# A clustered attention and a feed-forward layer on one core: five hand-over queues written in a new order

## The chip, the cores and the metric

The kernel runs on one core of one Trainium2 chip. The time is device time of that core in microseconds, the median of the runs shown; lower is better. A core has five instruction queues that run on their own and wait for each other by semaphores: TensorE (PE; its weight loads are PEld), VectorE (DVE), ScalarE (ACT), GpSimd (POOL) and SyncE (SP), which here issues nearly all transfers.

## The reference

For 4 batches and 8 heads of 768 tokens with 64 numbers each, every query and key is given to the nearest of 16 centroids; a query sees only keys of its own cluster. The attention's output (3072 rows of 512) goes through a feed-forward layer of width 1024.

```python
mask = q_assign[:, :, :, None] == k_assign[:, :, None, :]
scores = np.where(mask, scale * q @ k.T, -1e9)
attn = softmax(scores) ; x = (attn @ v) as rows of 512
h = x @ w_in
solu = h * softmax(h)
ln = (solu - mean) / np.sqrt(var + 1e-06) * g_ln
return ln @ w_out
```

## The kernel before

The 32 heads are taken as 16 pairs, named batch.pair (0.0 to 3.3). For a pair, queries and keys (side 0 and 1) are loaded, turned so that the head dimension lies on partitions, scored against the centroids, and written in bf16 with a one-hot cluster code below them. With the code in the contraction, a score of a foreign cluster lies so far below that its exponential is nothing; the mask costs no instruction of its own. Score blocks of 512 (in the first pair 384) columns go through three PSUM banks: TensorE writes a bank, ScalarE takes the exponential into one of nine SBUF tiles, TensorE multiplies these with the values, and VectorE divides by the row sums. There are 294 such banks. Each of 24 blocks of 128 rows then goes through the feed-forward layer. It is folded: the output weights are centred and scaled once (ce), so that a row block needs a maximum, an exponential with its sum, a product u, a transposing transfer of u, the variance, one factor alpha for each row, and a last scaling.

Nothing of the order is left to a scheduler. The kernel registers about 1800 small steps with `add(name, engine, cost, key, fn, needs, ...)`, and class `Weave` (L18) holds for each engine a text, `ORDER`, that gives the kinds of steps in queue order with repeat counts: `S3 V` is three score steps and a value step, each the next of its kind. A word such as `=ca0.1.1.1` names one step out of turn. `AWAY` names steps that run on another engine than their default. `run()` then walks the five queues and emits the instructions; the real waits come from the tiles that the instructions touch. An engine's queue is strict: an instruction that waits holds all behind it.

The steps that are spoken of below, by kind:

- `ld`, `lv` (L410, L413, L382, L539): loads of queries or keys, and of values. From batch 1 on, one side of a pair is loaded in four quarters (ld1.2.1.0, .1, .2, and the last, ld1.2.1). `lo`, `li` (L576, L560): loads of the output and input weights.
- `tp` (PE, L394) and `xa` (L401): in batch 0 the turning by TensorE and the copy out of PSUM. `xt` (DVE, L419): from batch 1 on, the turning by VectorE.
- `cl` (PE, L462), `tb`, `mx`, `oh`, `ot` (DVE, L471 to L506), `pl` (L518, L526; some by SyncE, L524), `bl` (memset, L535): cluster scores, their maximum, the one-hot code, and its placing. `zo` (L893) is one memset for it.
- `ca` (L443 on ScalarE, L445 and L447): cast of one head of queries or keys to bf16; ca1.3.1.1 is batch 1, pair 3, keys, second head. `cv` (L544): cast of values. `wi` (L563): cast of a quarter of the input weights. `z`, `sg`, `gs` are small preparations.
- `S` (PE, L613), `E` (ACT, L619), `V` (PE, L636), `N` (DVE, L648 and L661): scores, exponentials, values, division.
- For row block f: `tx` (SP, L691) turns x by a transfer; `h` (PE, L722, four steps, h2.1.0 is block 2, second half, first part); `hm` (DVE, L728), `ex` (ACT, L734), `u` (DVE, L741), `tu` (SP, L746, a transposing transfer), `bn` and `ag` (DVE, L752, L756), `at` and `al` (POOL, L762 to L771), `y` (PE, L786, four steps), `sc` (L801 on ScalarE, L803 on VectorE), `ou` (SP, L813). In the last blocks `ptx` and `ptu` turn on TensorE.

Two bindings matter for the order. The product u of block f frees a PSUM bank that h of block f+1, second half, writes, so the loop h, hm, ex, u runs through three engines. And one PSUM bank is shared by cl and y: it is handed on by tb or sc.

Of the kernel before, what the change touches and what calls it, by code (L numbers as in the profile page):

```python
# [22 lines left out]
class Weave:  # L23
# [3 lines left out]

    ORDER = {}
    ORDER["SP"] = """
        ld4 lv si ld4 lv lg ld4 lv2 ld4 lo2 ld4 lo ld3 lo ld3 li4 tx ld3 lv3 tx ld4 tu ld9 lv ld tu  # L30
        tx ld3 tu ld3 ou ld2 ou ld tu ld12 tu ld4 lv ld2 ou tx ld3 tu ou ld2 tx lv ld tu ld4 tx ld
        tu ou2 ld lv ld4 tu ld4 tu ld ou ld7 pl ou ld lv2 ld3 tu lv tx ou tu lv pl ld4 ou2 tx lv tu
        tx ou tu pl2 tu2 tx tu tx ou2 tx ou tu tx2 ou tu2 ou2 tu2 ou6
    """
    ORDER["POOL"] = """
        po z ca2 pl2 cv z bl pl2 ca z ca pl2 ca z2 ca3 cv ca cv ca pl3 sg ca cv2 pl3 ca2 gs pl ca cv
        ca wi ca pl2 wi3 bl ca pl2 cv at cv pl ca pl al bl at cv ca pl ca pl cv ca3 al at ca al ca
        at ca pl2 bl cv pl2 ca4 at ca2 al ca pl2 bl pl2 cv2 ca3 al at pl2 bl pl2 ca pl al ca3 at cv
        at pl ca pl2 ca2 pl al cv2 bl cv2 pl2 ca pl al pl at al at pl2 ca3 at al bl cv pl2 bl cv2
        ca3 pl5 al cv3 at al ca2 cv ca cv ca2 at ca2 pl ca al pl2 at2 pl3 at ca cv al at2 al2 at2 al  # L40
        at al3 at al2 at2 al2
    """
    ORDER["PE"] = """
        wm tp fl3 cp fl2 tp2 cl tp fl10 cl fl8 S3 tp2 S2 tp S cq S tp S2 tp2 S2 V3 S cl S tp2 V3 S gt S tp S
        tp S2 cl S2 V2 S V S2 tp S2 tp S2 V2 S V S2 cl S2 V2 S V2 S3 V S2 V2 S2 V S cl S3 su S2 V3 S
        V S3 V3 S2 V S su S2 V S V3 S3 me S3 V4 S3 cl S3 V4 S2 h S h S2 h S h S2 V3 S2 V h S h V S V
        S h S V S V S h S2 V3 S2 V h S2 h V2 S y3 S2 h3 S3 y V3 h V S2 V2 S cl S3 h2 S2 V3 S y2 S V
        h2 S V y2 S h S V h S2 h S y3 S2 y V3 h S3 cl V2 S V S y S2 y2 S3 V3 S y S2 V3 S2 cl S V S2
        V2 S h S2 V2 S V S h S2 V2 cl V2 S3 y2 S V S2 V y S2 y V2 S3 h2 S V h S h S2 V h S V S V y2
        S h V y2 S2 V S h3 S cl V S2 V2 S h V cl S3 h2 V y V S3 y2 V S h V3 S y S h S2 h2 S3 V2 y h  # L50
        S V S2 y V3 y S3 h3 y S3 V3 S h S V S V cl S V S h S cl V2 S3 y V2 S y S2 y V2 S3 h y V S3 V
        h V2 S3 cl S2 V2 S y3 S2 y S V3 S V S y S2 V S V3 S2 y2 S3 y V2 S2 h V2 S3 h3 S V S2 V y S V
        h2 V2 S y S2 y V y S h2 S3 cl h V S2 V3 S h V2 S3 h2 S y S2 V h S2 V y2 V4 S3 y h S2 h V h V
        S V S y2 S3 V3 h2 S2 h2 S2 y2 S V S h2 S V3 S2 h S h S2 V S y V2 S V y2 S2 h2 S2 h2 V2 S2 V2
        y S2 h V2 h V S2 h S V h S3 V2 h y S V y3 V h3 S2 y3 S2 y h2 V2 h y h y3 h V h V y4 h ptx h
        y4 h2 y3 h2 y ptu2 y6 ptu y ptu y5
    """
    ORDER["DVE"] = """
        cn cb xa ca tb mx oh ot pl2 tb mx oh ot xa3 bl cf cv xa zo xa2 tb ca mx oh gk N ot tb pl mx
        xa2 oh xa cv N ot tb pl N xt mx xt N oh ot tb pl2 ca N pl xt mx N sk oh N ot xt ce3 N tb ce5  # L60
        N hm mx N u oh ot bn N bn ag hm xt2 u N bn2 hm ag sc xt u N bn tb hm mx bn oh ag u xt bn ot
        xt N cv hm bn ag sc xt tb mx N u xt oh ot sc N bn2 xt ag xt tb N hm mx tb N oh ot u xt mx N
        bn oh bn xt hm ot ag N cv u bn2 xt hm tb mx u N tb oh mx hm ot bn2 oh ag u N sc ag hm bn ot
        u bn N xt2 ag xt2 hm tb N bl mx tb bn2 oh u N xt ag xt sc hm ot tb mx oh N bn sc N u bn N ag
        xt ot bn ca N mx sc oh hm u bn ag N xt hm bn2 bl tb u ot ag N hm mx bn2 u bn N oh ot hm bl2
        u ag N cv hm sc bn u N hm ag bn N bn u bn2 hm ag2 N bn u bn2 N ag hm bn u N ag hm bn2 u bn2
        hm sc u N ag2 bn tx hm bn sc u bn ag hm bn tu ag u2 bn2 ag sc
    """
    ORDER["ACT"] = """
        wa xa2 ca2 xa ca2 E12 xa2 E6 xa E58 ex E12 ex E8 ex E8 ex E3 sc E5 ca E2 ex E25 ex E9 sc E6  # L70
        ex E5 sc E2 ex E9 ex E8 ex E9 sc E6 ex E18 ex E21 ex E5 sc E3 ex E9 ex E7 sc E2 ex E7 ex E8
        ex E7 ex E6 sc E ex E2 sc E3 ex E2 sc ex sc ex sc ex tu sc tu2 sc2 oz
    """
    AWAY = {}
    AWAY.update(dict.fromkeys("""
        ca0.0.0.0.0 ca0.0.0.1.1 ca1.3.1.1 sc23.0 tu22.1 tu23.1 xa0.0.1.0 xa0.2.1.0 xa0.2.1.1
        xa0.3.0.0
    """.split(), "ACT"))
    AWAY.update(dict.fromkeys("""
        bl0.0.1 bl2.2 bl3.1 bl3.2 bl3.3 ca0.0.1.0.0 ca0.1.1.0 ca1.0.0.1 ca3.1.1.0 cv0.0.0 cv0.2.0  # L80
        cv1.2.0 cv2.0.0 cv3.3.0 pl0.0.0.0.1 pl0.1.0.0 pl0.2.1.1 pl0.3.0.0 pl0.3.0.1 pl0.3.1.0 sc0
        sc10 sc13 sc17 sc19 sc2 sc23.1 sc3 sc6 sc8 sc9 tu22.0 zo
    """.split(), "DVE"))
    AWAY.update(dict.fromkeys("""
        ca0.0.1.1.1 pl0.0.0.1.0 pl0.0.1.0.0 pl0.0.1.1.0 pl1.0.0.0 pl1.0.0.1 pl1.0.1.0 pl1.0.1.1
        pl1.1.0.0 pl1.1.0.1 pl1.1.1.0 pl1.1.1.1 pl1.2.0.0 pl1.2.0.1 pl1.2.1.0 pl1.2.1.1 pl1.3.0.0
        pl1.3.0.1 pl1.3.1.0 pl1.3.1.1 pl2.0.0.0 pl2.0.0.1 pl2.0.1.0 pl2.0.1.1 pl2.1.0.0 pl2.1.0.1
        pl2.1.1.0 pl2.1.1.1 pl2.2.0.0 pl2.2.0.1 pl2.2.1.0 pl2.2.1.1 pl2.3.0.0 pl2.3.1.0 pl2.3.1.1
        pl3.0.0.0 pl3.0.0.1 pl3.0.1.0 pl3.0.1.1 pl3.1.0.1 pl3.1.1.0 pl3.1.1.1 pl3.2.0.0 pl3.2.0.1
        pl3.2.1.0 pl3.3.0.1 pl3.3.1.0 pl3.3.1.1  # L90
    """.split(), "POOL"))
    HOP = 0.17
    LANES = 8
# [1178 lines left out]
```

## Time and profile before

| | |
|---|---|
| median of 3 runs | 225.22 us (224.92 to 555.72) |
| span of the profiled execution | 225.3 us |
| granted TensorE clock | 1.00 in the whole span |
| instructions profiled | 6672 |
| transfers | 38.80 MB, 172 GB/s in the mean |
| HBM read and written | 23.11 MB and 6.29 MB |

In the profile a row of a group gives line, engine, operation, output and inputs, shapes, the count, then busy microseconds and the mean nanoseconds of one, then the idle time of the engine just before these instructions and what ended it. A row of the timeline begins with the start and the length in microseconds. A row of the waits names who waited for whom, with the sum, the count and the longest. The ends of matmuls are modelled, and a releaser is inferred from semaphore events: where a wait was for several things, the last is named, and where the one named had long been done, it was another.

### The profile page before, as it was taken

How to read it: one execution, taken by the hardware profiler on the slowest of the kernel's cores; microseconds unless marked ns; L12 is line 12 of the kernel's file. 1: busy time of each engine (PE TensorE's matmuls, PEld its weight loads, DVE VectorE, ACT ScalarE, POOL GpSimd, SP SyncE). 2: the span in 40 equal slices, each digit the busy share in tenths (PEclk: the TensorE clock that was granted, in tenths of full speed). 3: DMA queues.
4: the chain of work that ended last, by engine and by line, in shares of the span. 5: the costliest groups of instructions: out<-in, count | busy, mean ns of one | idle time of the engine just before them, and what ended most of it. 6: DMA issues, size and time to landing. Idle time of an engine off the chain costs nothing.

```text
span 225.3 us, 6672 instructions
## 1 busy us (share of the span) xinstructions
PE 217.0 (96%) x2454; PEld 142.4 (63%) x2454; DVE 197.2 (88%) x359; ACT 191.9 (85%) x372; POOL 127.0 (56%) x247
## 2 busy tenths in 40 slices
PE   8999999999899999999999999999999999999994
PEld 7676646676556657666567657676566676755452
DVE  3899888899799998999998999887999889988982
ACT  3779978999969999998989899998899998984363
POOL 3499833684792999654667752855696502123331
PEclk9999999999999999999999999999999999999999
DMA  6998999999899899899999998887970637266923
GB/s 153 316 318 164 243 173 224 312 217 192 141 179 168 195 134 157 161 204 170 193 215 174 148 172 217 178 154 190 235 114 9 83 57 155 70 139 158 180 87 140
DMA packets 125679, 38.80 MB, mean 172 GB/s; under 512 B 115016, under 2 KB 121168, under 8 KB 125648
## 3 DMA queue, kind: packets, MB, share of 16 engines
q1 hardware_dynamic: 123904, 37.87, 83.0%
q10 hardware_dynamic: 1744, 0.52, 1.0%
q8 instruction: 19, 0.31, 0.6%
q14 instruction: 12, 0.10, 0.2%
HBM read 23.11 MB, written 6.29 MB: 130 GB/s over the span
## 4 chain that ended last, share of the span: by engine, by line
PE 73%; DMA 8%; DVE 7%; SPq 4%; ACT 3%; issue 3%; POOL 1%; DVEq 0%; ACTq 0%; POOLq 0%
PE sps L613 21%; PE hreg L722 16%; PE yps L786 15%; PE ops L636 11%; DMA raw<-in_k_dram 4%; PE csc L462 3%; SPq L413 3%; PE hreg L394 2%; ACT e L619 2%; DMA uT<-u 2%; DMA xT<-x 2%; PE idle_p L831 1%; DVE xt L419 1%; DVE u L741 1%; PE hreg L585 1%
## 5 line engine op out<-in xcount | busy, mean ns | idle before, releaser
L619 ACT ACTIVATE e<-sps 128x512 bf16<-128x512 f32 (+1 forms) x294 | 150.9, 601 | 14.6 <-PE sps L613 12.1
L613 PE MATMUL sps<-qk 80*128 80x256 bf16 (+5 forms) x636 | 93.7, 262 | 1.6 <-ACT e L619 0.6
L613 PEld LDWEIGHTS <-qk 80*128 80x128 bf16 (+1 forms) x636 | 51.7, 97 | 32.4 <-issue 9.4
L636 PEld LDWEIGHTS <-e 128*128 128x128 bf16 x1152 | 49.2, 97 | 13.0 <-issue 1.9
L722 PE MATMUL hreg<-w_in_sb,xT 128*128 128x512 bf16 x192 | 53.0, 379 | 1.4 <-DVE u L741 1.3
L636 PE MATMUL ops<-v,e 128*128 128x65 bf16 x1152 | 53.5, 193 | 0.1
L786 PE MATMUL yps<-w_out_c,uT 128*128 128x512 bf16 x184 | 48.7, 379 | 0.6 <-DMA uT<-u 0.4
L741 DVE TENSOR_TENSOR u<-e_sb,hreg 128x1024 bf16<-128x1024 bf16 (+1 forms) x25 | 29.1, 1167 | 4.6 <-ACT e_sb L734 4.5
L526 POOL COPY qk<-oht 32x384 f32<-32x384 f32 (+1 forms) x50 | 24.4, 488 | 15.3 <-DVE oht L506 12.6
L752 DVE BATCH_NORM_STATS2 bs<-u 128x6 f32<-128x512 bf16 x48 | 31.5, 676 | 0.1
L728 DVE TENSOR_REDUCE nmax<-hreg 128x1 f32<-128x1024 f32 x24 | 29.0, 1209 | 2.5 <-PE hreg L722 2.2
L734 ACT ACTIVATE e_sb<-hreg,nmax 128x1024 bf16<-128x1024 f32 x24 | 27.0, 1124 | 4.5 <-DVE nmax L728 4.4
L445 POOL CAST qk<-xt 64x768 bf16<-64x768 f32 (+1 forms) x31 | 25.9, 836 | 4.8 <-DVE xt L401 3.3
L786 PEld LDWEIGHTS <-uT 128*128 128x128 bf16 x200 | 18.1, 97 | 13.0 <-issue 0.7
L419 DVE STREAM_TRANSPOSE xt<-raw 128x768 f32<-128x768 f32 x24 | 22.9, 957 | 3.2 <-POOL v L544 1.5
L768 POOL TENSOR_SCALAR esq<-es,mv 128x1 f32<-128x1 f32 x24 | 8.6, 358 | 29.5 <-DVE mv L756 21.3
L722 PEld LDWEIGHTS <-xT 128*128 128x128 bf16 x192 | 16.5, 97 | 11.9 <-DVE u L741 2.3
L447 POOL TENSOR_SCALAR qk<-xt 64x768 bf16<-64x768 f32 (+1 forms) x28 | 22.9, 819 | 1.7
L661 DVE TENSOR_TENSOR x<-ops,den 128x256 bf16<-128x256 f32 (+1 forms) x39 | 18.9, 485 | 1.3
L762 POOL TENSOR_SCALAR es<-esum 128x1 f32<-128x1 f32 x24 | 5.3, 223 | 26.1 <-ACT e_sb L734 25.6
L544 POOL CAST v<-vf 128x384 bf16<-128x384 f32 x27 | 13.6, 518 | 2.9 <-DMA vf<-in_v_dram 2.3
L771 POOL TENSOR_TENSOR alpha<-esq,halves 128x1 f32<-128x1 f32 x24 | 13.5, 563 | 2.0
(80 smaller groups left out, 170.0 us busy)
## 6 DMA issues: line engine op xcount, KB each, us to landing
vf<-in_v_dram SPq DMA_DIRECT2D x16, 384.0 KB, 4.6
out_dram<-y SPq DMA_DIRECT2D x23, 256.0 KB, 2.4
raw<-in_q_dram SPq DMA_DIRECT2D x50, 96.0 KB, 3.7
raw<-in_k_dram SPq DMA_DIRECT2D x50, 96.0 KB, 3.5
w_g<-in_moe_w_out_dram SPq DMA_DIRECT2D x4, 512.0 KB, 6.2
w_st<-in_moe_w_in_dram SPq DMA_DIRECT2D x4, 512.0 KB, 6.0
raw<-in_q_dram SPq DMA_DIRECT2D x3, 384.0 KB, 6.6
raw<-in_k_dram SPq DMA_DIRECT2D x3, 384.0 KB, 7.3
```

What stands on the lines that cost most here:

```text
L419: nc.vector.transpose(xt[:], raws[b, p, i][:].rearrange("p j c -> p (j c)"))
L445: VEC[e].tensor_copy(dst, src)
L526: ins = VEC[e].tensor_copy(dst.bitcast(F32), src.bitcast(F32).unsqueeze(1) .to_broadcast([NB, 2, n // 2]))
L613: nc.tensor.matmul(sps_[n, k][:, c0:c0 + w], side(b, h // 2, 1, h % 2, keys)[r], side(b, h // 2, 0, h % 2, slice(s0 * P, s0 * P + w))[r])
L619: nc.scalar.activation(es[n, k][:, :w], sps_[n, k][:, :w], Act.Exp, scale=exp_scale, bias=-exp_scale)
L636: nc.tensor.matmul(opss[g][:, s, :VW], es[n, k][:, c0:c0 + P], v1[slot(b, h // 2)][:, h % 2, kt, :VW], start=(kt == 0), stop=(kt == n_t - 1))
L722: uses(nc.tensor.matmul(hreg[:, at(f, f2)[1], :], xTs[f][:, dc, :], w_in_sb[:, dc, f2 * FF2:(f2 + 1) * FF2], start=(dc == 0), stop=(dc == ...
L728: uses(nc.vector.tensor_reduce(ff[f, "nmax"][:], pair_of(f), axis=AXY, op=Alu.max, negate=True), *both(f))
L734: uses(nc.scalar.activation(ff[f, "e"][:], pair_of(f), Act.Exp, bias=ff[f, "nmax"][:], accum_out=ff[f, "esum"][:]), *both(f))
L741: uses(nc.vector.tensor_tensor(ff[f, "u"][:, at_], ff[f, "e"][:, at_], pair_of(f)[:, at_], op=Alu.mult), *banks)
L752: nc.vector.bn_stats(ff[f, "bs"][:, f2, :], ff[f, "u"][:, f2, :])
L786: ins = nc.tensor.matmul(dst, ff[f, "uT"][:, at(f, f2)[0] * (n_fc // 2) + c, :], w_out_c[:, fc, cols], start=(fc == chunks[0]), stop=(fc = ...
```

## The change

Only the texts `ORDER` and `AWAY` change. The steps, their code, the tiles and the number of buffers are the same. The queues keep their order until the first scores; behind these the order of all five is new, and it names steps out of turn (for GpSimd above all), which the texts before did not. By `AWAY`, ScalarE gains the casts ca0.1.0.0, ca0.2.0.1, ca1.2.1.0, ca2.1.1.0, ca2.3.0.0 and ca3.2.1.0 and gives up ca1.3.1.1 and the copies xa0.2.1.0 and xa0.2.1.1; of the last scalings it gains sc2, 3, 6 and 13 and gives up sc11, 12, 20 and 22, which go to VectorE. VectorE has wi3 and three whole placements in place of five, and six value casts in place of five; three memsets and zo go to GpSimd, which has 55 casts of queries and keys in place of 59. The queues of SyncE and ScalarE follow in full, the others by their beginning, and VectorE's end.

```diff
     ORDER["SP"] = """
-        ld4 lv si ld4 lv lg ld4 lv2 ld4 lo2 ld4 lo ld3 lo ld3 li4 tx ld3 lv3 tx ld4 tu ld9 lv ld tu
-        tx ld3 tu ld3 ou ld2 ou ld tu ld12 tu ld4 lv ld2 ou tx ld3 tu ou ld2 tx lv ld tu ld4 tx ld
-        tu ou2 ld lv ld4 tu ld4 tu ld ou ld7 pl ou ld lv2 ld3 tu lv tx ou tu lv pl ld4 ou2 tx lv tu
-        tx ou tu pl2 tu2 tx tu tx ou2 tx ou tu tx2 ou tu2 ou2 tu2 ou6
+        ld4 lv si ld4 lv lg ld11 lv2 lo4 ld7 li4 tx lv2 tx ld7 tu lv ld8 lv tx tu2 ou ld12 tu ou2
+        ld10 tu ld4 lv tx tu ld6 ou tx ld4 lv tu2 ou2 tx lv ld13 tu ld6 ou pl ld2 lv tu2 ou ld lv
+        ld3 tx ld2 tu ou tx pl ou ld pl ld lv2 tu ou tu lv ou tx pl ou tu2 tx2 ou tx tu2 tx ou2 tu
+        tx ou tu2 ou2 tu ou5
     """
     ORDER["POOL"] = """
-        po z ca2 pl2 cv z bl pl2 ca z ca pl2 ca z2 ca3 cv ca cv ca pl3 sg ca cv2 pl3 ca2 gs pl ca cv
-        ca wi ca pl2 wi3 bl ca pl2 cv at cv pl ca pl al bl at cv ca pl ca pl cv ca3 al at ca al ca
...
+        po z ca2 pl2 bl ca sg pl2 bl cv =ca0.1.1.1 cv =cv0.1.1 =ca0.1.1.0 zo ca z2 =ca0.2.1.0 gs
+        =pl0.1.0.0 pl2 cv ca =pl0.2.0.1 pl =z5 =pl0.2.0.0 ca pl ca2 cv2 =ca0.3.1.1 ca pl2 =pl1.0.1.1
+        wi =ca1.0.0.1 wi2 =ca1.1.1.1 ca z =pl1.0.0.1 =ca1.1.0.0 cv =pl1.0.0.0 pl bl ca =pl1.1.1.1 pl
+        bl pl =ca1.2.0.0 cv =ca1.1.1.0 =cv1.2.0 pl at2 al2 cv =ca1.3.0.0 ca cv =ca1.2.1.1 =cv1.3.0
...
     ORDER["PE"] = """
-        wm tp fl3 cp fl2 tp2 cl tp fl10 cl fl8 S3 tp2 S2 tp S cq S tp S2 tp2 S2 V3 S cl S tp2 V3 S gt S tp S
-        tp S2 cl S2 V2 S V S2 tp S2 tp S2 V2 S V S2 cl S2 V2 S V2 S3 V S2 V2 S2 V S cl S3 su S2 V3 S
-        V S3 V3 S2 V S su S2 V S V3 S3 me S3 V4 S3 cl S3 V4 S2 h S h S2 h S h S2 V3 S2 V h S h V S V
...
+        wm tp fl3 cp fl2 tp2 cl tp fl10 cl fl8 S3 tp2 cq S2 tp S tp S2 tp S tp S tp V3 S2 cl S V3 S2
+        gt tp S tp S2 cl S2 V S V2 S2 tp S3 V2 S V S tp S2 tp S V2 S2 V2 S2 cl S3 V4 S3 cl S V S2 V2
+        S V S2 su S V S V S V2 S3 su S V S2 V3 S2 me S3 cl S3 V3 S V S3 V2 S V S V S2 h S h2 S h S V
...
     ORDER["DVE"] = """
-        cn cb xa ca tb mx oh ot pl2 tb mx oh ot xa3 bl cf cv xa zo xa2 tb ca mx oh gk N ot tb pl mx
-        xa2 oh xa cv N ot tb pl N xt mx xt N oh ot tb pl2 ca N pl xt mx N sk oh N ot xt ce3 N tb ce5
-        N hm mx N u oh ot bn N bn ag hm xt2 u N bn2 hm ag sc xt u N bn tb hm mx bn oh ag u xt bn ot
...
-        hm sc u N ag2 bn tx hm bn sc u bn ag hm bn tu ag u2 bn2 ag sc
+        cn cb xa ca tb mx oh ot pl2 tb mx oh ot xa3 =pl0.0.1.0.1 xa cf pl =xa0.2.1.0 xa2 tb mx N gk
+        xa oh ot tb mx pl oh ot N xa3 xt N cv xt tb mx N oh tb ot ca N cv pl2 mx oh N ot sk xt N xt
+        ce tb ce2 N ce2 wi ce N ce2 hm mx oh N u bn N ot hm xt bn N u bn ag bn xt hm ag sc xt u N tb
...
+        bn ag bn u bn ag N hm bn ag u bn2 hm sc N u ag bn2 hm tx ag sc u bn2 hm tu sc ag u2 bn2 ag
+        sc2
     """
     ORDER["ACT"] = """
-        wa xa2 ca2 xa ca2 E12 xa2 E6 xa E58 ex E12 ex E8 ex E8 ex E3 sc E5 ca E2 ex E25 ex E9 sc E6
-        ex E5 sc E2 ex E9 ex E8 ex E9 sc E6 ex E18 ex E21 ex E5 sc E3 ex E9 ex E7 sc E2 ex E7 ex E8
-        ex E7 ex E6 sc E ex E2 sc E3 ex E2 sc ex sc ex sc ex tu sc tu2 sc2 oz
+        wa xa2 ca2 xa ca2 E9 ca E3 ca E6 xa E58 ex E11 ex E11 ex E3 ca E7 ex E6 sc E3 ex sc E12 sc
+        E13 ex E11 sc E3 ex E =ca2.3.0.0 E2 sc E2 ex ca E8 ex E3 sc E7 ex E6 sc E11 ex E17 ex E21 ex
+        E8 ex E3 ca E5 ex E9 ex E8 ex E7 sc ex E7 ex E2 sc E5 ex E2 sc E3 ex sc E ex sc ex2 tu sc
+        tu2 sc oz
     """
     AWAY = {}
...
-        ca0.0.0.0.0 ca0.0.0.1.1 ca1.3.1.1 sc23.0 tu22.1 tu23.1 xa0.0.1.0 xa0.2.1.0 xa0.2.1.1
-        xa0.3.0.0
+        ca0.0.0.0.0 ca0.0.0.1.1 ca0.1.0.0 ca0.2.0.1 ca1.2.1.0 ca2.1.1.0 ca2.3.0.0 ca3.2.1.0 sc23.0
+        tu22.1 tu23.1 xa0.0.1.0 xa0.3.0.0
     """.split(), "ACT"))
...
-        bl0.0.1 bl2.2 bl3.1 bl3.2 bl3.3 ca0.0.1.0.0 ca0.1.1.0 ca1.0.0.1 ca3.1.1.0 cv0.0.0 cv0.2.0
-        cv1.2.0 cv2.0.0 cv3.3.0 pl0.0.0.0.1 pl0.1.0.0 pl0.2.1.1 pl0.3.0.0 pl0.3.0.1 pl0.3.1.0 sc0
-        sc10 sc13 sc17 sc19 sc2 sc23.1 sc3 sc6 sc8 sc9 tu22.0 zo
+        bl1.2 bl2.1 ca0.0.1.0.0 ca1.0.1.0 ca3.2.0.1 cv0.2.1 cv0.3.1 cv2.3.1 cv3.0.0 cv3.1.0 cv3.2.1
+        pl0.0.0.0.1 pl0.0.1.0.1 pl0.1.0.1 pl0.3.0.1 pl0.3.1.1 sc0 sc10 sc11 sc12 sc17 sc19 sc20 sc22
+        sc23.1 sc8 sc9 tu22.0 wi3
     """.split(), "DVE"))
```

## What the change does to the time: the prediction

> **What bounds the kernel now.** I read the page's totals first, then TensorE's groups with the shapes kept apart, a short stretch of its timeline, the busy times by stage, and last the waits.
>
> ```profile
> span 225.3 us, 6672 instructions
> PE 217.0 (96%) x2454; PEld 142.4 (63%) x2454; DVE 197.2 (88%) x359; ACT 191.9 (85%) x372; POOL 127.0 (56%) x247
> ...
> L636 PE MATMUL ops<-v,e 128*128 128x65 bf16 x1152 | 53.5, 193 | 0.1
> L722 PE MATMUL hreg<-w_in_sb,xT 128*128 128x512 bf16 x192 | 53.0, 379 | 1.4 <-DVE u L741 1.3
> L786 PE MATMUL yps<-w_out_c,uT 128*128 128x512 bf16 x184 | 48.7, 379 | 0.6 <-DMA uT<-u 0.4 <-DVE cst L471 0.2
> L613 PE MATMUL sps<-qk 80*128 80x256 bf16 x288 | 47.5, 272 | 1.1 <-ACT e L619 0.6
> L613 PE MATMUL sps<-qk 96*128 96x256 bf16 x180 | 29.5, 272 | 0.0
> ...
> 150.34 0.53 PE L636 MATMUL ops<-v,e 128*128 128x65 bf16 x12
> 150.70 0.60 PE L613 MATMUL sps<-qk 80*128 80x256 bf16 x4
> 151.14 0.60 PE L722 MATMUL hreg<-w_in_sb,xT 128*128 128x512 bf16 x2
> ```
>
> The mean length of a matmul holds a tail that the next one overlaps. Two of 512 columns take 0.60 together and 0.379 alone, so the second starts 0.22 after the first; four of 256 columns give (0.60 - 0.272) / 3 = 0.11, and twelve value matmuls (0.53 - 0.193) / 11 = 0.031. In such slots the three large kinds need 376 x 0.22 + 468 x 0.11 + 1152 x 0.031 = 83 + 51 + 35 = 169 us; the other 458 matmuls (transposes, clusters, warming) come on top. So TensorE is the fullest engine, though a gap shorter than the tail is hidden in its 217.
>
> ```profile
> 9.40:55.40 46.00, 44.69 (x544) 29.66 (x545) 41.16 (x84) 41.81 (x88) 30.43 (x54) 1.00 0.97 237
> 55.40:66.00 10.60, 9.28 (x108) 6.27 (x107) 8.98 (x15) 8.35 (x17) 8.64 (x15) 1.00 0.83 141
> 66.00:200.00 134.00, 133.10 (x1576) 88.54 (x1575) 122.88 (x212) 124.83 (x239) 77.65 (x146) 1.00 0.86 155
> 200.00:225.30 25.30, 21.93 (x154) 11.66 (x151) 19.52 (x31) 12.11 (x21) 7.08 (x18) 1.00 0.57 142
> ...
> PE hreg L722 <- DVE u L741: 1.3, 1, 1.3
> ...
> ACT e L619 <- PE sps L613: 12.1, 23, 2.1
> ```
>
> After the stretch and its length the columns are PE, PEld, DVE, ACT, POOL, then the granted clock, which is 1.00 throughout: no term comes from it. From 66 to 200 TensorE is busy 133.1 of 134.0, ScalarE 124.8, VectorE 122.9. Three engines are nearly full and hand work to each other in queues of fixed order. TensorE's visible waits are few: one of 1.3 us, and in the groups above 0.6 for exponentials and 0.4 for a transfer. ScalarE's 12.1 us are its wait for scores, so it is the one that has room, in many small pieces.
>
> **The one wait that the new order plainly removes.** It stands in the second stretch.
>
> ```profile
> 54.39 2.35 SPq L746 DMA_TRANSPOSE uT<-u  x1
> 56.79 0.59 SPq L413 DMA_DIRECT2D raw<-in_k_dram  x1
> ...
> 58.87 0.27 ACT L734 ACTIVATION_READ_ACCUMULATOR e_sb<-hreg,nmax 128x1 f32 x1
> ...
> 60.01 0.98 DVE L419 STREAM_TRANSPOSE xt<-raw 128x768 f32<-128x768 f32 x1 [1.55 <-POOL v L544]
> 60.92 1.18 DVE L741 TENSOR_TENSOR u<-e_sb,hreg 128x1024 bf16<-128x1024 bf16 x1
> ...
> 62.16 1.04 PE L722 MATMUL hreg<-w_in_sb,xT 128*128 128x512 bf16 x4 [1.32 <-DVE u L741]
> ```
>
> The last quarter of a key load leaves SyncE at 56.79, because the transposing transfer tu0 held the queue for 2.35 us ahead of it. VectorE stands 1.55 us before xt1.2.1 (the view names GpSimd, whose cast has nothing to do with that tile; the load is the likely releaser). u1 is queued behind it, though its exponentials were done at 58.87 + 0.27 = 59.14, and h2.1.0 on TensorE waits for u1. The new VectorE queue reads xt1.2.0 bn0.1 N11 u1 bn1.0 ag0 bn1.1 xt1.2.1: u1 no longer stands behind the load. It could start at 59.14 rather than 60.92, 1.78 earlier, against a wait of 1.32. **Term: -1.3** (bounds -1.3 and 0; the near end, since the gain exceeds the wait). Late next there would be h2.1.0 itself, by the time that bn0.1 and N11 delay u1; between h1.1.1 and h2.1.0 TensorE's new order has one score more to do, which covers 0.2 us.
>
> **Work that changes its engine.**
>
> ```profile
> L801 ACT ACTIVATE y<-yps,alpha 128x512 f32<-128x512 f32 x13 | 9.0, 695 | 5.7 <-PE yps L786 5.4 <-POOL alpha L771 0.3
> L401 ACT COPY xt<-hreg 128x384 f32<-128x384 f32 x6 | 2.8, 478 | 1.4 <-PE hreg L394 1.4
> L443 ACT ACTIVATE qk<-xt 64x768 bf16<-64x768 f32 x1 | 0.8, 841 | 0.0
> L401 DVE COPY xt<-hreg 128x384 f32<-128x384 f32 x10 | 5.1, 537 | 0.9 <-PE hreg L394 0.9
> L518 DVE COPY qk<-w_out_c 16x384 f32<-16x384 f32 x5 | 2.3, 458 | 0.2
> L544 DVE CAST v<-vf 128x384 bf16<-128x384 f32 x5 | 2.2, 437 | 0.0
> L535 DVE MEMSET qk<- 16x384 f32 x4 | 1.5, 378 | 0.4
> L447 DVE TENSOR_SCALAR qk<-xt 64x768 bf16<-64x768 f32 x2 | 1.0, 520 | 0.0
> L563 POOL CAST w_in_sb<-w_st 128x1024 bf16<-128x1024 f32 x4 | 4.0, 1038 | 5.5 <-DMA w_st<-in_moe_w_in_dram 5.4
> ```
>
> ScalarE gains six whole casts (ca0.1.0.0, ca0.2.0.1, ca1.2.1.0, ca2.1.1.0, ca2.3.0.0, ca3.2.1.0), loses one (ca1.3.1.1) and two copies xa0.2.1.x: 5 x 0.841 - 2 x 0.478 = +3.25 us. Four scalings sc come (2, 3, 6, 13) and four go (11, 12, 20, 22), so at 0.695 each ScalarE has 2.1 us more by sc6 and gives it back late. Bounds for the time: 0, if the casts fall into its waits (134.0 - 124.8 = 9.2 us idle from 66 to 200), and +3.25, if each pushes the exponentials and through them the scores. I take a quarter, **+0.8**: nearer to 0, because TensorE is the fuller of the two in that stretch (133.1 against 124.8); not 0, because only three score banks lie between the two engines, and ScalarE's idle time is scattered among its 23 waits for scores.
>
> VectorE: two copies xa (+1.07), one value cast net (+0.44), wi3 (bounded by its four on GpSimd, 1.04, and by 0.437 x 1024 / 384 = 1.17 on VectorE itself; I take 1.0), two small and minus two large placements (under 0.5 either way), minus two whole memsets and a half one (-0.9), minus one cast (-0.52), minus zo, a memset too (about -0.4 by that row). Sum about +0.7, 0.4 per cent of its 197: **0**, hidden by its own idle time of 134.0 - 122.9 = 11 us; without that cover +0.7. GpSimd loses four casts, a value cast and wi3 net and gains three memsets and zo; at 127 of 225 busy it bounds no stage: **0**. What counts of it is which operation stands at its head, below.
>
> [...]
>
> **The order of the queues.** On TensorE the multiset is the same, so its slots are too. SyncE: lv0.2 and lv0.3 move behind seven more quarter loads; their casts' consumers (V8.0 and later) come after 33 us, far off. The four lo move together ahead of seven quarters of pair 1.1; li0 to li3 keep places 36 to 39. tu2 and ou0 move ahead of the last quarter of ld1.3.1 and of pair 2.0, the tightest spot I found (rival C). GpSimd: the small per-token steps at and al move behind casts for pairs further ahead (at0 behind cv1.2.0 and pl1.1.0.1), so casts are ready earlier and scalings have less lead; sc0 is the first to feel it. VectorE's late queue: bn22.1 moves ahead of hm23, sc20 comes between tu22.0 and ag22, and sc22 goes behind ag23.
>
> ```profile
> 220.40 0.69 ACT L801 ACTIVATE y<-yps,alpha 128x512 f32<-128x512 f32 x1
> 220.49 0.21 DVE L756 BATCH_NORM_AGGREGATE mv<-bs 128x2 f32<-128x12 f32 x1
> 221.82 0.47 ACT L801 ACTIVATE y<-hreg,alpha 128x256 f32<-128x256 f32 x1 [0.74 <-POOL alpha L771]
> ```
>
> At the end sc22 ran on ScalarE from 220.40 to 221.09; on VectorE it can start at 220.49 + 0.21 = 220.70, while alpha of the last row block lets the last scaling start at 221.82 either way. **Tail: 0** (up to +0.3 if sc22 delays sc23.1). The first 9.4 us keep their order: **0**.
>
> The other visible waits (0.6 for exponentials, 0.4 for a transfer) may go, and others as large may come: bounds -1.0 and +1.0. I take **-0.6**: in the first third of the scores, stretches of TensorE work over 1 us between two scores fall from six to two (counted from the two orders in the slots above), and such a stretch is what lets ScalarE run dry.
>
> Sum, on the profiled execution: 225.3 - 1.3 + 0.8 + 0 + 0 - 0.6 = **224.2**. That execution is 0.1 above the median of 225.22; the difference is not carried.
>
> **Rivals.**
> A, faster. In 9.4 to 55.4 ScalarE is busy 41.8 of 46.0. If the more even order let it run through, the stage would last 41.8 + 2 x 0.841 - 2 x 0.478 = 42.5, 3.5 less, and the whole 225.3 - 1.3 - 3.5 = 220.5. For it: the 12.1 us of waits for scores. Against: TensorE is busy 44.7 there by the same row, and part of those waits are the cluster chains. [...] Chance 0.08.
>
> B, ScalarE as the bound. All +3.25 lands on the path, since each cast stands between exponentials, and the waits for scores come back after it: 225.3 - 1.3 + 3.25 = 227.3, still within 2%. Chance 0.14.
>
> C, slower: a transfer that waits for u2 holds the loads behind it.
>
> ```profile
> 60.22 2.69 SPq L413 DMA_DIRECT2D raw<-in_k_dram  x4
> 64.44 2.21 SPq L746 DMA_TRANSPOSE uT<-u  x1
> 70.75 1.36 SPq L746 DMA_TRANSPOSE uT<-u  x1
> 66.65 1.21 DVE L741 TENSOR_TENSOR u<-e_sb,hreg 128x1024 bf16<-128x1024 bf16 x1
> 73.39 0.97 DVE L419 STREAM_TRANSPOSE xt<-raw 128x768 f32<-128x768 f32 x1
> ...
> raw<-in_k_dram SPq DMA_DIRECT2D x50, 96.0 KB, 3.5
> ```
>
> The last quarter of ld1.3.1 is the fourth of the pieces at 60.22, and xt1.3.1 ran at 73.39. In the new queue it stands behind tu2, which left at 70.75, and ou0. If tu2 leaves no earlier, the quarter leaves about 72.8; it lands 3.5 us later by the page's table of transfers (last row), at 76.3, 2.9 late, and the loads of pair 2.0 behind it repeat that once: 224.2 + 2 x 2.9 = 230.0. Against: tu2 waits for u2 only, which was over at 66.65 + 1.21 = 67.86, 2.9 before tu2 left; and hm4 behind xt1.3.1 serves an h5 that lies far off. It decides when xt1.3.1 starts after about 77. Chance 0.12.
>
> **How the numbers follow.** Forecast 0.66, A 0.08, B 0.14, C 0.12. A 2% step is 4.5 us (below 220.7, above 229.7), about what a measurement of this kernel can tell from no change: faster 0.08, same 0.66 + 0.14 = 0.80, slower 0.12. The range leaves out A and C. Its high end is B with other waits 1.0 worse, 228.3; its low end is the forecast with the casts hidden (-0.8) and half of A's early gain (-1.75), 221.7.
>
> **What would show it.** Right: no wait of h2.1.0 near 62 and u1 ahead of its load; ScalarE about 195 busy; the scores' stage until 55 no longer than 46; xt1.3.1 before 75; the last scaling released by alpha as before. Wrong: waits of TensorE for exponentials summing to over 2 us near the moved casts (B), VectorE standing before xt1.3.1 or xt2.0.0 (C), or the first stage near 42.5 (A).

## The result, and the profile after

| | median of the runs | lowest to highest | ratio to before, 95% interval |
|---|---|---|---|
| before, first runs | 225.22 us | 224.36 to 225.66, and one of 555.72, unexplained | |
| after, first runs (7) | 223.60 us | 223.06 to 223.91 | 0.9938 [0.9909, 0.9968] |
| after, on another chip (6) | 223.61 us | 223.30 to 224.88 | 0.9884 [0.9842, 0.9925] |

The changed kernel is 0.6 to 1.2 per cent faster, which is less than 2%. Beside the experiments the kernel before ran 81 times more on three chips; its medians there are 226.57, 226.91 and 226.85 us, and its runs go from 224.23 to 230.80. The 13 runs of the changed kernel lie between 223.06 and 224.88, so it also spreads less. The ratios leave out runs over 1.5% above a kernel's fastest and the medians do not, so where a kernel spreads the two differ, and the ratio is the safer.

In the profiled execution of after the span is 221.0 us and the time of the same run is 223.14; a second profile of before has a span of 224.5 and a time of 226.41. About 2 us lie outside the span. The execution of before on which the prediction rested (span 225.3) was therefore one of some 227.3 us, 2 above the median, and not 0.1 above it. By spans the profiles differ by 4.3 us, of which the median of the first runs shows 1.6.

The page of after, its totals and TensorE's and ScalarE's groups (line numbers are those of before plus 8):

```profile
span 221.0 us, 6663 instructions
PE 214.6 (97%) x2454; PEld 141.6 (64%) x2454; DVE 198.7 (90%) x358; ACT 193.3 (87%) x375; POOL 124.1 (56%) x245
...
L627 ACT ACTIVATE e<-sps 128x512 bf16<-128x512 f32 (+1 forms) x294 | 149.7, 602 | 7.1 <-PE sps L621 5.5
...
L730 PE MATMUL hreg<-w_in_sb,xT 128*128 128x512 bf16 x192 | 54.0, 378 | 0.0
L794 PE MATMUL yps<-w_out_c,uT 128*128 128x512 bf16 x184 | 49.5, 379 | 0.0
```

TensorE's idle time fell from 225.3 - 217.0 = 8.3 to 221.0 - 214.6 = 6.4. Its busy time fell by 2.4 with the same 2454 matmuls; the likely reason, which was not shown, is that gaps shorter than a matmul's tail (0.379 - 0.22 = 0.16 us at 512 columns, by the slots of the prediction), which count as busy, became fewer. ScalarE does 1.4 us more and waits 5.5 for scores in place of 12.1.

The waits of after, TensorE's alone (total, times, longest):

```profile
PE idle_p L839 <- DVE halves L843: 1.0, 1, 1.0
PE sps L621 <- DVE qk L534: 0.4, 1, 0.4
PE hreg L402 <- DMA raw<-in_q_dram: 0.4, 1, 0.4
PE ops L644 <- DVE x L669: 0.2, 1, 0.2
```

Apart from the warming matmuls at the start (the first row) no wait that this view names is longer than 0.4 us. The wait for u (1.3 us in before), the two for exponentials (0.6) and the one for a transfer (0.4) are gone.

The busy times by stage:

```profile
9.40:55.40 46.00, 44.81 (x561) 30.25 (x562) 42.69 (x86) 43.23 (x90) 31.04 (x54) 1.00 0.91 234
55.40:66.00 10.60, 10.60 (x125) 7.11 (x122) 10.03 (x16) 10.60 (x22) 7.96 (x17) 1.00 0.97 165
66.00:200.00 134.00, 133.87 (x1584) 89.18 (x1583) 124.58 (x212) 127.68 (x244) 76.82 (x147) 1.00 0.80 159
```

The first stage is as full as it was. The second has no idle time left on TensorE, where before had 10.60 - 9.28. From 66 on TensorE's idle time fell from 0.90 to 0.13. Exponentials come in the same sequence in both kernels, so their starts can be set against each other: of the 294 (counted from 0), number 84 starts 0.6 us earlier than before, number 168 3.7, and the last 3.6; the rest of the 4.3 lies behind it.

The timeline of after where before had the wait of 1.32 us, and where rival C would have been seen:

```profile
58.29 1.21 DVE L749 TENSOR_TENSOR u<-e_sb,hreg 128x1024 bf16<-128x1024 bf16 x1
60.81 0.96 DVE L427 STREAM_TRANSPOSE xt<-raw 128x768 f32<-128x768 f32 x1
73.41 0.96 DVE L427 STREAM_TRANSPOSE xt<-raw 128x768 f32<-128x768 f32 x1
...
60.19 0.59 PE L730 MATMUL hreg<-w_in_sb,xT 128*128 128x512 bf16 x2
...
63.22 4.05 SPq L754 DMA_TRANSPOSE uT<-u  x2
67.32 0.57 SPq L821 DMA_DIRECT2D out_dram<-y  x1
67.95 0.63 SPq L421 DMA_DIRECT2D raw<-in_k_dram  x1
```

u1 runs at 58.29 ahead of xt1.2.1, and h2.1.0 starts at 60.19 without a wait, 1.97 earlier. tu1 and tu2 leave one behind the other from 63.22, so that the last quarter behind them leaves at 67.95; xt1.3.1 starts at 73.41, as before (73.39).

### The profile page after: what moved, and what is told of

Its sections match the earlier page's. It is cut to its first block, busy times and chain, and to the rows that moved or that the text cites. A ratio compares the mean times of both kernels' runs of the same rounds, so it can differ in the third digit from the quotient of the medians.

```text
span 221.0 us, 6663 instructions
## 1 busy us (share of the span) xinstructions
PE 214.6 (97%) x2454; PEld 141.6 (64%) x2454; DVE 198.7 (90%) x358; ACT 193.3 (87%) x375; POOL 124.1 (56%) x245
## 4 chain that ended last, share of the span: by engine, by line
PE 87%; DVE 5%; ACT 3%; DMA 2%; issue 1%; SPq 1%; ACTq 0%; DVEq 0%
PE sps L621 27%; PE yps L794 18%; PE hreg L730 17%; PE ops L644 14%; PE csc L470 4%; ACT e L627 3%; PE hreg L402 2%; DMA raw<-in_q_dram 2%; PE csc L465 1%; PE hreg L593 1%; PE hreg L794 1%; DVE nmax L736 1%; DVE xt L409 1%; DVE u L749 1%; DVE oh L504 0%
## 5 line engine op out<-in xcount | busy, mean ns | idle before, releaser
L621 PE MATMUL sps<-qk 80*128 80x256 bf16 (+5 forms) x636 | 98.9, 262 | 1.2 <-DVE qk L534 0.4
L621 PEld LDWEIGHTS <-qk 80*128 80x128 bf16 (+1 forms) x636 | 50.2, 97 | 33.6 <-issue 12.1
L644 PEld LDWEIGHTS <-e 128*128 128x128 bf16 x1152 | 50.9, 97 | 11.8 <-DVE x L669 1.1
L644 PE MATMUL ops<-v,e 128*128 128x65 bf16 x1152 | 55.3, 193 | 0.3 <-DVE x L669 0.2
L730 PE MATMUL hreg<-w_in_sb,xT 128*128 128x512 bf16 x192 | 54.0, 378 | 0.0
L794 PE MATMUL yps<-w_out_c,uT 128*128 128x512 bf16 x184 | 49.5, 379 | 0.0
L534 POOL COPY qk<-oht 32x384 f32<-32x384 f32 (+1 forms) x48 | 23.6, 491 | 27.5 <-DVE oht L514 22.0
L453 POOL CAST qk<-xt 64x768 bf16<-64x768 f32 (+1 forms) x28 | 22.9, 821 | 4.8 <-DVE xt L409 3.5
L730 PEld LDWEIGHTS <-xT 128*128 128x128 bf16 x192 | 17.6, 97 | 8.9 <-DVE u L749 0.4
```

What stands on the lines that cost most here:

```text
L453: VEC[e].tensor_copy(dst, src)
L534: ins = VEC[e].tensor_copy(dst.bitcast(F32), src.bitcast(F32).unsqueeze(1) .to_broadcast([NB, 2, n // 2]))
L621: nc.tensor.matmul(sps_[n, k][:, c0:c0 + w], side(b, h // 2, 1, h % 2, keys)[r], side(b, h // 2, 0, h % 2, slice(s0 * P, s0 * P + w))[r])
L644: nc.tensor.matmul(opss[g][:, s, :VW], es[n, k][:, c0:c0 + P], v1[slot(b, h // 2)][:, h % 2, kt, :VW], start=(kt == 0), stop=(kt == n_t - 1))
L730: uses(nc.tensor.matmul(hreg[:, at(f, f2)[1], :], xTs[f][:, dc, :], w_in_sb[:, dc, f2 * FF2:(f2 + 1) * FF2], start=(dc == 0), stop=(dc == ...
L794: ins = nc.tensor.matmul(dst, ff[f, "uT"][:, at(f, f2)[0] * (n_fc // 2) + c, :], w_out_c[:, fc, cols], start=(fc == chunks[0]), stop=(fc = ...
```

## Experiments

**The kernel before again, and u1 alone.** The first has no edit. The second moves one word on VectorE.

> The kernel before, profiled once more. My theory (the wait of h2.1.0 for u1, behind a late load, belongs to the order): ratio 1.00 within 0.3%, span about 223 to 225, and again VectorE standing about 1.5 us before xt1.2.1 and TensorE about 1.3 us before h2.1.0. Rival (the first profile was an execution with an unusually late load): span near 223.1, since the changed kernel's span lies 2.1 below its time, and no such wait, or one under 0.5 us.

```diff
     ORDER["DVE"] = """
...
-        N hm mx N u oh ot bn N bn ag hm xt2 u N bn2 hm ag sc xt u N bn tb hm mx bn oh ag u xt bn ot
+        N hm mx N u oh ot bn N bn ag hm xt u xt N bn2 hm ag sc xt u N bn tb hm mx bn oh ag u xt bn ot
```

> The kernel before with one exchange in VectorE's queue: u1 ahead of xt1.2.1. My theory: the wait of h2.1.0 goes, 1.3 us, ratio 0.994, which is the whole of the measured gain. Rival 1 (the late load was of that one execution): ratio 1.000 within 0.2%. Rival 2 (the gain comes from the evener order of the first stage or of the late part): ratio 0.998 to 1.000.

Before again: 226.41 us, ratio 1.0015 [0.9966, 1.0065]; there the wait of h2.1.0 was 0.7 us, not 1.3. u1 first: 228.68 us, ratio 1.0101 [1.0028, 1.0174], slower. Its trace (SyncE's queue, then TensorE, then its waits):

```profile
93.77 2.47 SPq L691 DMA_TRANSPOSE xT<-x  x1
...
97.12 0.82 PE L613 MATMUL sps<-qk 96*128 96x256 bf16 x6
99.64 0.82 PE L722 MATMUL hreg<-w_in_sb,xT 128*128 128x512 bf16 x3 [1.70 <-DMA xT<-x]
...
PE hreg L722 <- DMA xT<-x: 1.7, 1, 1.7
PE idle_p L831 <- DVE halves L835: 1.0, 1, 1.0
PE yps L786 <- DMA uT<-u: 0.9, 1, 0.9
```

And the same transfer, tx6, in before, with the matmuls that need it:

```profile
95.34 1.76 SPq L691 DMA_TRANSPOSE xT<-x  x1
...
98.69 0.82 PE L613 MATMUL sps<-qk 96*128 96x256 bf16 x6
99.60 1.04 PE L722 MATMUL hreg<-w_in_sb,xT 128*128 128x512 bf16 x4
```

The wait at 62 is gone, and the exponentials lead those of before by 1.0 at number 84, 2.5 at number 93 and 2.1 at number 108. The first 1.0 was there at 55 us, ahead of the edit, and is of that execution; the edit itself brought the 1.5 behind it. But x of block 6 is there at 99.6 in both kernels (in before the weight load of h6 waits 0.36 for it until 99.60): tx6 left 1.57 earlier and took as much longer. h6 then waits 1.70, and at number 156 the lead is 0.05 the other way. The win was real and was given back 38 us later. That leaves the mean time without a gain. A part of why it is a per cent worse than before is the granted clock: three of the six runs have a mean of 0.985 to 0.993, and they are the longest (229.51 to 231.35 us). The other three, at 1.00, have a median of 227.14, still above before; the one trace, which is one of these, does not show why.

**Half of the change: the new order until 67 us and the old one behind it, and the reverse.** All five queues are spliced. SyncE's begin is shown for the first.

```diff
     ORDER["SP"] = """
-        ld4 lv si ld4 lv lg ld4 lv2 ld4 lo2 ld4 lo ld3 lo ld3 li4 tx ld3 lv3 tx ld4 tu ld9 lv ld tu
-        tx ld3 tu ld3 ou ld2 ou ld tu ld12 tu ld4 lv ld2 ou tx ld3 tu ou ld2 tx lv ld tu ld4 tx ld
...
+        ld4 lv si ld4 lv lg ld11 lv2 lo4 ld7 li4 tx lv2 tx ld7 tu lv ld8 lv tx tu ld5 tu ld3 ou ld2 ou
+        ld tu ld12 tu ld4 lv ld2 ou tx ld3 tu ou ld2 tx lv ld tu ld4 tx ld tu ou2 ld lv ld4 tu ld4 tu
...
```

> The new order for all steps until about S30.0 (a little behind h2.1.0), the old order for the steps that are left. My theory: the whole gain lies here, ratio 0.991 to 0.994, since the later casts on ScalarE are left out. Rival (the gain is spread over the kernel or lies in the late part): 0.997 to 1.000, with a loss at the seam possible.

> The old order until about S30.0, the new one for the steps that are left. My theory: no gain, a small loss by the four casts that ScalarE has more there (up to 0.8 us), ratio 1.000 to 1.004. Rival (the gain is spread or late): 0.995 to 0.998.

New then old: 226.81 us, ratio 1.0006 [0.9957, 1.0055]. Its exponentials led by 4.0 us at number 96, 2.0 at 108, 0.6 at 120 and 0.1 at 156; a part of the first figure is only work of the feed-forward that comes later. Lost by waits of 1.8 for uT and 0.6 for xT. Old then new: 224.23 us, ratio 0.9950 [0.9908, 0.9991], and there TensorE still waits 0.6 for u. So the gain is not won where I looked for it, in the first 67 us, but kept or lost behind them.

**The changed kernel, and the changed kernel with SyncE's old queue.** The first has no edit; its ratio of 0.9884 (the table above) is below the range that was expected. The second puts the SP text of before back.

> The changed kernel once more, as the measure on this chip. All theories: ratio 0.991 to 0.997 as before, with less spread than the kernel before if its lead over the transfers is larger.

```diff
     ORDER["SP"] = """
-        ld4 lv si ld4 lv lg ld11 lv2 lo4 ld7 li4 tx lv2 tx ld7 tu lv ld8 lv tx tu2 ou ld12 tu ou2
...
+        ld4 lv si ld4 lv lg ld4 lv2 ld4 lo2 ld4 lo ld3 lo ld3 li4 tx ld3 lv3 tx ld4 tu ld9 lv ld tu
...
```

> The changed kernel with SyncE's old queue. New theory (the transfers pace the middle: what the other queues win before 95 us is lost again at h6, which waits for tx6, and tx6 stands behind loads in the old queue): the gain goes, ratio 0.999 to 1.004, with TensorE waiting for xT or uT for 1 us or more. Rival (the gain is in the order of the other four engines): 0.992 to 0.996.

225.77 us, ratio 0.9941 [0.9902, 0.9981], beside 0.9884 [0.9842, 0.9925] for the changed kernel on the same chip: 0.0057 or 1.3 us slower by the ratios, 2.2 by the medians. TensorE waits as my theory says, but the ratio lies in the rival's range: about half of the gain on that chip stays without SyncE's order. That a part goes with it shows in the runs: five of the six of the changed kernel are shorter than all twelve of this one. TensorE's waits, and the place of the longest with its transfer, in an execution of 227.85 us, one of the four longest:

```profile
PE hreg L730 <- DMA xT<-x: 2.3, 2, 1.3
PE yps L794 <- DMA uT<-u: 1.9, 2, 1.7
...
141.18 2.57 SPq L754 DMA_TRANSPOSE uT<-u  x1
...
147.37 0.39 PE L794 MATMUL yps<-w_out_c,uT 128*128 128x512 bf16 x1 [1.69 <-DMA uT<-u]
```

tu10 leaves at 141.18, behind two loads of values and the quarters of ld3.3.0, and y of block 10 waits for it until 147.37. In the changed kernel it left about 5.4 us earlier. The others of the three stand at 70.55 (tx4, 1.29) and 100.32 (tx6, 0.98). Set beside the changed kernel's trace, the exponentials fall back by 1.3 us at the first of these places, by 0.9 at the one at 100 and by 1.9 at the one at 147, and by 0.4 twice elsewhere (near 31 and near 106 us). That makes up the 5.0 us between the two spans (226.0 and 221.0); the median execution lost less than half of it.

**One transfer at a time in the kernel before.** To u1 first are added tx6 ahead of the last two quarters of ld2.3.0, and then, in a second kernel, ou2 too. SyncE's lines, from u1 first to the second:

```diff
...
-        tx ld3 tu ld3 ou ld2 ou ld tu ld12 tu ld4 lv ld2 ou tx ld3 tu ou ld2 tx lv ld tu ld4 tx ld
-        tu ou2 ld lv ld4 tu ld4 tu ld ou ld7 pl ou ld lv2 ld3 tu lv tx ou tu lv pl ld4 ou2 tx lv tu
...
+        ld3 tu ld3 ou ld2 ou ld tu ld12 tu ou ld4 lv tx ld5 tu ou ld2 tx lv ld tu ld4 tx ld tu ou2 ld
+        lv ld4 tu ld4 tu ld ou ld7 pl ou ld lv2 ld3 tu lv tx ou tu lv pl ld4 ou2 tx lv tu tx ou tu pl2
...
```

> The kernel before with u1 ahead of xt1.2.1 as in u1_first, and on SyncE tx6 ahead of the last two quarters of ld2.3.0 and of ou2. New theory: the 1.6 us that u1_first had won by 90 us and lost at h6 are kept, ratio 0.992 to 0.996. Rival (h6 waits for the division N17 and the transfer's own length, not for the queue): as u1_first, 1.00 to 1.01.

> The kernel before with u1 ahead of xt1.2.1, tx6 ahead of the last two quarters of ld2.3.0, and ou2 ahead of the last two quarters of ld2.2.1. Theory (what u1 wins is lost to the transfers of block 6 and to the store of block 2, both now early): about 1.5 us of the win are kept past bank 156, and the time is 0.992 to 0.997 of before. Rival (the old queue is full, and each transfer made early makes a later one late): 1.000 to 1.012, the win lost at another transfer before bank 200.

With tx6: 229.18 us, ratio 1.0140 [1.0081, 1.0199]. With ou2 as well: 227.52, ratio 1.0028 [0.9975, 1.0081]. From the first of them (ScalarE, then TensorE):

```profile
100.30 0.69 ACT L800 ACTIVATE y<-yps,alpha 128x512 f32<-128x512 f32 x1 [2.92 <-DMA out_dram<-y]
...
101.52 0.38 PE L612 MATMUL sps<-qk 80*128 80x256 bf16 x2 [2.70 <-ACT e L618]
```

tx6 was early now, but the store of block 2 stood behind it. Scaling sc4 reuses that block's output tile, waits 2.92 for the store, and holds ScalarE's queue, so TensorE waits 2.70 for exponentials. With ou2 moved as well this wait is gone, and the ratio is 0.011 lower (on another chip), but not below 1. A part of that may be the granted clock: three of the six runs with tx6 alone have a mean of 0.992 or 0.993, and none of the twelve with ou2 as well is under 0.997. The trace with ou2 moved as well has another wait of 1.48 at 48.24 for tx0, whose place nobody had changed; in before it landed 5.6 us after its issue, and h0 started at 46.79 without a wait. Two repairs were not enough; my theory said that they would be.

**Four old places made early, under the new orders of the other engines.** The kernel with SyncE's old queue, and in it tx4 ahead of the loads of pair 2.0, ou2 and tx6 as above, and tu10 ahead of lv2.3.

```diff
-        ld4 lv si ld4 lv lg ld4 lv2 ld4 lo2 ld4 lo ld3 lo ld3 li4 tx ld3 lv3 tx ld4 tu ld9 lv ld tu
-        tx ld3 tu ld3 ou ld2 ou ld tu ld12 tu ld4 lv ld2 ou tx ld3 tu ou ld2 tx lv ld tu ld4 tx ld
-        tu ou2 ld lv ld4 tu ld4 tu ld ou ld7 pl ou ld lv2 ld3 tu lv tx ou tu lv pl ld4 ou2 tx lv tu
...
+        ld4 lv si ld4 lv lg ld4 lv2 ld4 lo2 ld4 lo ld3 lo ld3 li4 tx ld3 lv3 tx ld4 tu ld9 lv tx ld tu
+        ld3 tu ld3 ou ld2 ou ld tu ld12 tu ou ld4 lv tx ld5 tu ou ld2 tx lv ld tu ld4 tx ld tu ou2 ld
+        lv ld4 tu ld4 tu ld ou ld7 pl ou ld tu lv2 ld3 lv tx ou tu lv pl ld4 ou2 tx lv tu tx ou tu pl2
...
```

> The changed kernel with SyncE's old queue, in which only four steps are moved: tx4 ahead of the loads of pair 2.0, ou2 ahead of the last two quarters of ld2.2.1, tx6 ahead of the last two quarters of ld2.3.0, tu10 ahead of lv2.3. Theory (a few small transposing transfers that stood behind loads carried what the old queue lost, 2.2 us of 226 against the changed kernel): the three waits of TensorE at 70, 100 and 147 us go, and the time is 0.987 to 0.991 of before, within 0.7 us of the changed kernel. Rival (the spacing of the whole new queue matters): 0.993 to 0.998, with the lost time turned into other waits for transfers.

224.93 us (224.40 to 226.21), ratio 0.9955 [0.9920, 0.9991], in the rival's range. The three waits are gone, and one is new:

```profile
99.26 1.31 SPq L752 DMA_TRANSPOSE uT<-u  x1
...
102.48 0.60 PE L792 MATMUL yps<-w_out_c,uT 128*128 128x512 bf16 x2 [1.17 <-DMA uT<-u]
```

tu5, behind six quarters that follow it in the new queue, leaves at 99.26 instead of 94.5, and y of block 5 waits 1.17. Up to number 156 the exponentials of this trace are 0.5 us behind those of the changed kernel, from number 161 on 1.8, and at the end 1.9, which is the distance of the spans (222.9 and 221.0): most of what is left is this one place. By the medians the kernel stays 1.3 us behind the changed one (two chips). Beside the old queue its ratio is no lower (0.9955 and 0.9941, two chips); what is gone is the spread (1.8 us in place of 4.8). So the waits named are real, but that their removal lowers the usual time is not shown: the next late transfer took their place.

**Two transfers late in the changed kernel.** ou2 and tx6 go behind ld2.3.0.

```diff
     ORDER["SP"] = """
-        ld4 lv si ld4 lv lg ld11 lv2 lo4 ld7 li4 tx lv2 tx ld7 tu lv ld8 lv tx tu2 ou ld12 tu ou2
-        ld10 tu ld4 lv tx tu ld6 ou tx ld4 lv tu2 ou2 tx lv ld13 tu ld6 ou pl ld2 lv tu2 ou ld lv
...
+        ld4 lv si ld4 lv lg ld11 lv2 lo4 ld7 li4 tx lv2 tx ld7 tu lv ld8 lv tx tu2 ou ld12 tu ou ld10
+        tu ld4 lv tu ld3 ou tx ld3 ou tx ld4 lv tu2 ou2 tx lv ld13 tu ld6 ou pl ld2 lv tu2 ou ld lv ld3
...
```

> The changed kernel with ou2 and tx6 moved back behind ld2.3.0, where the old queue has them. Theory (their places carry a part of the gain): h6 waits for tx6 or a scaling waits for the store of block 2, and the time is 0.5 to 1.5 us above the changed kernel's 0.988, so 0.990 to 0.995 of before. Rival (it is the sum of many small leads, not these two): 0.986 to 0.990.

230.57 us (230.11 to 233.61), ratio 1.0198 [1.0135, 1.0260]: 7.0 us slower than the changed kernel by the medians (of two chips), against 0.5 to 1.5 expected. SyncE's queue and TensorE:

```profile
91.26 0.66 SPq L545 DMA_DIRECT2D vf<-in_v_dram  x1
94.86 1.26 SPq L752 DMA_TRANSPOSE uT<-u  x1
96.17 2.90 SPq L416 DMA_DIRECT2D raw<-in_q_dram  x3
99.17 0.47 SPq L819 DMA_DIRECT2D out_dram<-y  x1
99.69 1.29 SPq L697 DMA_TRANSPOSE xT<-x  x1
...
103.32 1.89 PE L728 MATMUL hreg<-w_in_sb,xT 128*128 128x512 bf16 x4 [5.39 <-DMA xT<-x]
```

In the changed kernel tx6 left at 91.96. It now stands behind tu5, which is not free until u5 is done (94.86), behind three loads, and behind the store ou2. It leaves at 99.69, and h6 waits 5.39 us. In the old queue tx6 stands ahead of tu5, so this place is later than in either queue, and the 7.0 us are not the price of the old place. The granted clock gives the rest (windows, as above):

```profile
90.00:97.90 7.90, 7.90 (x112) 5.45 (x110) 7.45 (x15) 7.90 (x17) 4.51 (x8) 1.00 0.75 154
97.90:103.30 5.40, 0.03 (x1) 0.00 (x0) 1.84 (x4) 1.67 (x4) 3.81 (x8) 0.66 0.85 159
103.30:106.00 2.70, 2.68 (x13) 1.37 (x14) 0.39 (x2) 0.00 (x0) 0.00 (x0) 0.50 1.04 223
106.00:109.00 3.00, 3.00 (x22) 1.68 (x21) 1.85 (x4) 2.12 (x4) 0.00 (x0) 0.92 0.95 159
```

While TensorE stood, the clock fell from 1.00 to 0.50, and the 5.7 us behind the wait ran at 0.50 and 0.92: 2.70 x 0.50 + 3.00 x 0.08 = 1.6 us. The four matmuls behind the wait show it: they take 1.89, where four of before took 1.04 (at 99.60, above). By this estimate the place costs 5.4 + 1.6 = 7.0 us; between the two traces the exponentials fall back 7.1 here.

**ScalarE's casts back to GpSimd.** First the four late casts that ScalarE gained (ca1.2.1.0, ca2.1.1.0, ca2.3.0.0, ca3.2.1.0), then all but ca2.1.1.0, each ahead of the other head of its pair. `AWAY`, from the changed kernel to the second:

```diff
-        ca0.0.0.0.0 ca0.0.0.1.1 ca0.1.0.0 ca0.2.0.1 ca1.2.1.0 ca2.1.1.0 ca2.3.0.0 ca3.2.1.0 sc23.0
-        tu22.1 tu23.1 xa0.0.1.0 xa0.3.0.0
+        ca0.0.0.0.0 ca0.0.0.1.1 ca0.1.0.0 ca0.2.0.1 ca2.1.1.0 sc23.0 tu22.1 tu23.1 xa0.0.1.0 xa0.3.0.0
```

> The changed kernel with the four later casts of ScalarE (ca1.2.1.0, ca2.1.1.0, ca2.3.0.0, ca3.2.1.0) back on GpSimd, ahead of their pair's other head. My prediction's term: ScalarE's casts cost a quarter of their time, so 0.6 to 0.8 us faster than the changed kernel (0.996 of it, 0.990 of the kernel before). Rival B: up to 2.5 us faster (0.983). Other rival (ScalarE's waits for scores hide them, GpSimd holds up its small steps): the same or slower than the changed kernel.

> The changed kernel with three of the four late casts that ScalarE gained (ca1.2.1.0, ca2.3.0.0, ca3.2.1.0) back on GpSimd, ahead of the other head of their pair; ca2.1.1.0, whose return made TensorE wait, stays on ScalarE. Theory (the casts lie in ScalarE's waits for scores and cost nothing): the same as the changed kernel within 0.5 us, 0.986 to 0.991 of before. The prediction's term (a quarter of 0.84 each): 0.6 us faster. Rival B (each cast wholly on the path): 2.5 us faster, 0.977. Slower by over 0.5 would say that GpSimd is the engine that these casts would hold up.

Four back: 226.73 us, ratio 0.9999 [0.9957, 1.0041], slower than the changed kernel on the same chip by 0.0115 or 2.6 us by the ratios, 3.1 by the medians. Three back: 223.94 us, ratio 0.9934 [0.9897, 0.9972], within 0.4 of the changed kernel's two medians. From the trace with four back (GpSimd, then TensorE):

```profile
111.36 0.50 POOL L549 CAST v<-vf 128x384 bf16<-128x384 f32 x1 [2.12 <-DMA vf<-in_v_dram]
111.93 0.82 POOL L450 CAST qk<-xt 64x768 bf16<-64x768 f32 x1
112.83 2.08 POOL L452 TENSOR_SCALAR qk<-xt 64x768 bf16<-64x768 f32 x2
...
114.07 0.39 PE L618 MATMUL sps<-qk 80*128 80x256 bf16 x2 [1.77 <-POOL qk L452]
```

And from the changed kernel's (ScalarE's cast ca2.1.1.0, then GpSimd at the same cast of values):

```profile
107.29 0.83 ACT L451 ACTIVATE qk<-xt 64x768 bf16<-64x768 f32 x1
110.88 0.50 POOL L552 CAST v<-vf 128x384 bf16<-128x384 f32 x1 [2.19 <-DMA vf<-in_v_dram]
```

GpSimd stood 2.12 us at a cast of values whose load had not landed, with both heads of ca2.1.1 behind it, and TensorE waited 1.77 for the first. The changed kernel stands 2.19 at the same cast, but there ScalarE had made ca2.1.1.0 at 107.29, early enough. So the wait is not new; the cast was put behind it. The exponentials fall back 1.95 us against the changed kernel's at this point. The medians show more, since six of the twelve runs with four back have a mean granted clock of 0.983 to 0.992 (227.20 to 232.43 us); the other six have a median of 225.17, and with three back no run is under 0.998. One cast on the queue that is busy 56% of the time was dear; three on the queue that is busy 87% were free, as far as two chips can be compared.

## Why the prediction was right, step by step

The time (224.2 forecast, 223.6 measured) and the class were right. The sum that led there was not.

- **The order of SyncE's queue, costed at 0: this is the step that failed.** It carries 1.3 us by the ratios (2.2 by the medians), about half of the gain on that chip. The prediction went through that queue looking for a place where the new order is worse and found none that costs, but it did not look for places where the old one was late. The traces name tx4, tx6, tu5 and tu10 and the store ou2, small transfers behind quarters of loads for pairs far ahead. What each is worth in the usual execution was not separated, and with four of them early the ratio did not fall.
- **-1.3 for u1's place: the mechanism is right, the credit is not.** The wait went as described. Alone the edit gains nothing (1.0101), because the prediction asked what would be late next within a microsecond of h2.1.0, and the next late thing was tx6, 38 us on. The wait itself was 0.7 in another execution. And the kernel with the old order until 67 us keeps the wait (0.6) and is still faster than before (0.9950).
- **+0.8 for ScalarE's casts: mis-sized.** Three of the four late casts measure 0.3 us or less, with the other sign: three back did not gain (two chips; the other three were not tested by themselves). The cover that the prediction named, ScalarE's waits for scores, held; they fell by 6.6 us.
- **GpSimd at 0: right for its busy time, wrong for its queue.** With ca2.1.1.0 back, behind a wait for values that the new order has in any case, TensorE waits 1.8 us; the medians differ by 2.8 (226.73 against 223.94, two chips), a part of it by the granted clock. In before this cast was on GpSimd and TensorE had no such wait; so it is a property of the new order that ScalarE must take it.
- **-0.6 for other waits: right in kind.** Those for exponentials (0.6) and for uT (0.4) went.
- **Tail and first 9 us at 0: right.** In the timeline of after sc22 runs on VectorE at 216.38 and the last scaling of ScalarE is released by alpha at 217.57.
- **The base.** The sum starts from a span and was set beside a median of times; 2 us lie between them. As a span, 224.2 stands against 221.0 measured, so 3.2 us of gain were missing from the sum, and the 2 us left out hid the greater part of that. That 224.2 came so close to 223.6 is luck.

Rival A falls: the first stage is as long as it was. B falls with the casts. C falls where it was put, because tu2 left 4.7 us earlier; but its mechanism, a transfer that waits for u and holds what is behind it, is a part of what delays tx6 in the kernel with tx6 late (from 91.96, where it left in the changed kernel, to 94.86, of 7.7 us; the rest is tu5 itself, three loads and a store). The part of the gain that SyncE's order does not carry (ratio 0.9941 with the old queue, about half) was not divided among the other engines, so its cause stays open.

## What to carry to other kernels

In a queue that several streams share, list for each small transfer that the compute engine will need soon what stands ahead of it, and what those steps wait for in turn. A wait removed early counts only if every later transfer can keep up with the earlier schedule (with u1 first 2.5 us of lead at number 93 were gone at 156); follow the lead to the end, by the start of the same instruction in both traces. And judge a move to another engine by what stands at the head of that engine's queue at that moment, not by its busy share (behind a wait of 2.12 us for values, on the queue that was busy 56% of the time, one cast made TensorE wait 1.77).

## What the runs showed of the hardware that I had not expected

A stand of TensorE of 5.4 us cost, by the estimate above, 1.6 us more in granted clock. The kernel with tx6 late in finer windows:

```profile
97.90:99.00 1.10, 0.03 (x1) 0.00 (x0) 1.10 (x3) 0.98 (x3) 0.05 (x1) 1.00 0.77 122
99.00:99.50 0.50, 0.00 (x0) 0.00 (x0) 0.50 (x1) 0.00 (x0) 0.46 (x2) 1.00 0.22 23
99.50:100.00 0.50, 0.00 (x0) 0.00 (x0) 0.24 (x2) 0.00 (x0) 0.49 (x1) 0.68 0.55 91
100.00:101.00 1.00, 0.00 (x0) 0.00 (x0) 0.00 (x0) 0.00 (x0) 0.92 (x3) 0.50 1.13 325
...
106.00:106.50 0.50, 0.50 (x2) 0.15 (x1) 0.22 (x1) 0.44 (x1) 0.00 (x0) 0.50 1.16 220
106.50:107.00 0.50, 0.50 (x4) 0.20 (x3) 0.00 (x0) 0.16 (x1) 0.00 (x0) 1.00 0.40 75
```

The clock goes from 1.00 to 0.50 at about 99.7, 1.8 us into the stand, and back to 1.00 at 106.5, 3.2 us after work resumed. It was 1.00 behind shorter stands in the other traces: 1.69 us with SyncE's old queue, 1.70 with u1 first, 1.77 with four casts back, and 2.70 with tx6 added to u1 first. What sets the moments of the fall and of the return was not shown. All six runs of this kernel have a mean clock of 0.978 to 0.985. Runs of other kernels have lower clocks too, though none of them was profiled: six of twelve with four casts back (0.983 to 0.992), three of six each with u1 first (0.985 to 0.993) and with tx6 added to it (0.992 and 0.993). In the kernel before these are 8 of the 81 runs (0.991 to 0.993, 227.74 to 229.62 us). So the clock explains a part of its spread and not all: its two longest runs on one chip (229.75 and 230.21) and the longest on another (230.80) have a mean clock of 1.00.

The time from issue to landing of the same transfer differs between the traces: tx6 took 4.2 us in before, 3.7 in the changed kernel, and some 5.8 with u1 first (from 93.77 until h6 stops waiting at 99.64); tx0 took 5.6 in before and 4.2 in the changed kernel, and with ou2 moved as well, where SyncE's queue up to there is that of before, h0 waits 1.48 for it. That a queue without lead turns this into spread would fit the runs (224.2 to 230.8 us for before, 223.1 to 224.9 for the changed kernel) and was not tested.
